# Planner ranks and times, and a few early operations, in an attention and gated-MLP kernel ordered by a list scheduler

## The chip, the cores and the metric

The kernel runs on one core of a Trainium2 chip. The metric is the device time in microseconds (us). One core has TensorE (PE, matrix products; PEld is its weight load), VectorE (DVE), ScalarE (ACT), GpSimd (POOL) and SyncE (SP, which only issues transfers here). Each engine works through its own list of instructions in order, and waits by semaphores for what other engines or transfers deliver.

## What is computed

Eight batches of attention with 8 heads of 64: 32 global rows see all 544 keys, 512 local rows see the 32 global keys and a window of 32 to either side. The result, 4352 rows of 512, goes through two matrix products with a hard-swish gate between them.

```python
k_all = np.concatenate([k_g, k_l], axis=2)
v_all = np.concatenate([v_g, v_l], axis=2)
out_g = np.matmul(sm(scale * q_g @ k_all.T), v_all)             # 32 rows a head
mask = np.abs(pos[:, None] - pos[None, :]) <= 32
s_l = np.concatenate([scale * q_l @ k_g.T, np.where(mask, scale * q_l @ k_l.T, -1e9)], axis=-1)
out_l = np.matmul(sm(s_l), v_all)                               # 512 rows a head
x = np.concatenate([out_g, out_l], axis=2).transpose(0, 2, 1, 3).reshape(8 * 544, 512)
h = x @ w_in                                                    # 512 -> 2048
g = h * np.clip(h + 3.0, 0.0, 6.0) / 6.0
return g @ w_out                                                # 2048 -> 512
```

(shortened; `sm` is a softmax, all in float32)

## The kernel before

**Tiling.** Work goes by batch. q and k are cast to 16 bits and turned so that the head dimension lies on partitions: batch 0 by `stage_loads`, where half comes over SP's queue as float32 and is cast by ScalarE or VectorE (L431), the other half by casting loads from POOL's queue; batch 1 by two casting loads on POOL's queue (into `xt` and `qtmp`); batches 2 to 7 by `wide_loads`. The turns are VectorE transposes in `turn_words` (batches 0 and 1: L590 q, L595 k, L601 and L605 global q and k) and `turn_wide` (the others). The global rows of batches 0 and 1 come through `once`: a load, then four casts each for q and k (L478 and L480). Batch 1's load is issued by SP into `graw0`.

**Local attention** (`local`) handles four groups a batch, each with two units of 32 rows in two halves for all heads: scores (stream `s`, 64 matmuls, L712 for batches 0 and 1, L699 for the rest), mask and row minimum (`mx`, eight VectorE operations, L743), exponentials (`ex`, L749), eight transposes (`t`, L758), their copy from PSUM (`etc`, L318, on either engine), values (`av`, L776), normalisation (`nm`, L785 and L786) and a turn into `xt` (`xp`, L799). The values read `vs`, shifted copies ("strips") of v and of the global v: POOL, ScalarE or VectorE copy them for batch 0, POOL alone for the others (stream `vs`, L540 and L542). `globe` does the 32 global rows.

**Products** (`first`, `second`). For each batch the first product (L907) writes PSUM tiles `m` (three), ScalarE computes the clipped part (`t1`, L918), VectorE multiplies (`gate`, L914) into `gts` and so frees the tile. The second product (L934) works on groups of four matmuls; its result is copied (`ot`) and stored by SP. Batch 0's first product goes over its columns in three parts, of 128, 128 and 256. A batch's attention is held until the first product has come far enough (`hold`).

**Order.** Nothing is issued as the code is read. Every operation goes into a named stream of a `Plan`, with its engine (or a choice of engines), a planned duration, its dependencies and the buffers that it takes and reads. `Plan.lay` is a list scheduler: each stream keeps its own order; among the first operations of all streams it takes the one that can start soonest on its engine, and among those within 0.03 us the one of lowest rank. Where an operation may go on two engines, a free engine that no better-ranked operation wants is taken. The order so found is the order of the instructions on every engine. Planned dependencies fix only this order: at run time an engine waits only for real data dependencies. A load has an issue (on SP, POOL or ACT) and a planned service and flight (`lat`) on one DMA line; at most 8 loads of an engine are out at once. TensorE's operations cost 1.9 times as much before 30 us, and the planner follows its instructions in blocks of 256, of which the next is fetched (L179) while one is worked on:

```python
past = self.count % self.BLOCK + op.n - self.BLOCK
...
return max(0.0, self.fetched - at), at
...
if self.stalls(op, start, cost - self.switch(op))[0] > 0.2:
    rank += 20
```

`n` is the number of instructions: 128 for the scores of one local group in batches 0 and 1, 8 for a group of either product. The streams and their ranks stand at L296, the tiny matmuls that run first (`pad`) at L996. In the code, times of the plan count from its own start, and `when` is the planned time at which a block is used up.

Of the kernel before, what the change touches and what calls it, by code (L numbers as in the profile page):

```python
# [37 lines left out]
class Plan:  # L38
# [83 lines left out]
    def lay(self):  # L122
# [4 lines left out]
        while len(order) < total:  # L127
            found, lone = [], []
            for n, ops in self.streams.items():
                if at[n] == len(ops):  # L130
                    continue
                op = ops[at[n]]
                t = self.ready(op, n)
# [23 lines left out]
            first = min(found)  # L157
# [16 lines left out]
            if e == "PE":  # L174
                wait, when = self.stalls(op, start, self.cost(op, e, start))
                end += wait
                self.mode = op.mode[1]
                if self.count % self.BLOCK + op.n >= self.BLOCK:
                    self.fetched = when + wait + (7.0 if when < 40.0 else 5.2)  # L179
                self.count += op.n  # L180
# [12 lines left out]
def kernel(  # L193
# [102 lines left out]
    for name, rank in (("l0", 0), ("ld", 5), ("lq", -2), ("sh", 0), ("sq", 0), ("st", 3.5), ("g0", 0), ("ga", -9), ("first", -9), ("pad", -30), ("gc", -6), ("gd", 3), ("gp", 3.9), ("cast", -5), ("msk", lambda n: 1 if n < 9 else 1.25), ("tq", lambda n: 0 if n < 8 else 3), ("kg", 0.5), ("vs", 1.5), ("clr", 1),  # L296
                       ("s", 0.5), ("mx", lambda n: 1.2 if n < 33 else 2.7), ("ex", 1.9), ("t", -0.5), ("etc", 0), ("av", -0.7), ("nm", 0.7),
                       ("xp", -0.5), ("gx", 1),
                       ("mf", lambda n: 9 + n * 1e-3), ("ms", lambda n: 9 + (n + len(PARTS) * NDFF + 2) * 1e-3), ("t1", 0), ("gate", -0.7), ("ot", 3)):
        plan.stream(name, rank)  # L300
# [96 lines left out]
    def raw(src, b):  # L397
        return src[b].rearrange("h s d -> (h s d)").rearrange("(c x f) -> x c f", x=P, f=T * D)
# [17 lines left out]

    def stage_loads():
# [3 lines left out]
        there = [[load("g0", "SP", 0.47, 0.65, stage[:, i, c, :], raw(src, 0)[:, c, :], lat=(2.6, 3.1, 3.2, 5.7)[2 * c + i]) for i, src in enumerate((q_l, k_l))]  # L421
# [19 lines left out]
        for m in (2, 3, NU, 1, 0, NU + 1):  # L441
            made["mask", m] = [plan.add("msk", Op(("ACT", 0.21), lambda o=o, i=i: nc.scalar.copy(out=o, in_=i), [lower])) for o, i in places(m)]
# [23 lines left out]
    def once(b, k, src, name):  # L466

        raw_ = (graw0[:, k] if b else ots[k][0:W].rearrange("g (h d) -> g h d", d=D))
        got = load("sh" if b else "ga", "SP" if b else "ACT", 0.47, 0.45 if b else 0.3, raw_, src[b].rearrange("h g d -> g h d"), [w_in_l[1][1]] if b else ())
# [91 lines left out]
    def load_w_in():  # L561

        n = dff // 2
        rows = moe_w_in.rearrange("(k p a) c -> k p a c", k=2, a=2)
        got = [load("l0", "POOL", 0.7, 2.7, w_in_t[i][:, 2 * k:2 * k + 2, :], rows[k, :, :, i * n:(i + 1) * n])
               for i in range(2) for k in range(2)]
        return [got[0:2], got[0:2], got[2:4], got[2:4]]
# [16 lines left out]
    def turn_words(b, st, k):  # L584
# [4 lines left out]
        def turn_q(c0, c1):  # L589
            nc.vector.transpose(out=flat(qt[k.slot])[:, c0:c1].rearrange("p c (q t) -> p c t q", t=T), in_=words(nat(b, 0)[:, c0:c1]))  # L590
# [24 lines left out]
        for q in range(n):  # L615
# [10 lines left out]
            else:  # L626
                st["k"].append(plan.add("tq", Op(("DVE", 1.9 / n), lambda c0=c0, c1=c1: turn_q(c0, c1), st["qk"][q, 0],
                                                 [] if b == 0 else [k])))
                a = plan.add("tq", Op(("DVE", 1.95 / n), lambda c0=c0, c1=c1: turn_k(c0, c1), st["qk"][q, 1]))
                st["k"].append(a)  # L630
# [363 lines left out]
    with tc.manual_schedule():  # L994
        clean = plan.add("first", Op(("DVE", 0.1), lambda: nc.vector.memset(zero, 0.0)))
        plan.add("pad", Op(("PE", 4.0), lambda: [nc.tensor.matmul(out=aps[0][0:W, 0, 0:2], lhsT=zero, rhs=zero[:, 0:2], start=True, stop=True) for _ in range(100)], [clean],  # L996
# [83 lines left out]
```

## Time and profile before

| | |
|---|---|
| time, median of 3 runs | 327.46 us (327.25 to 327.77) |
| the profiled execution | 328.56 us, its span 326.8 us |
| PE busy in the span | 305.8 us (94%), 4484 matmuls |
| DVE, ACT, POOL busy | 258.4 (79%), 238.3 (73%), 157.7 us (48%) |
| mean DMA rate, bytes moved | 121 GB/s, 39.54 MB |
| chain that ended last | PE 86%, POOL 5%, DMA 3%, DVE 2%, issue 2% |
| granted TensorE clock, mean | 0.999 |

The span reaches from the first to the last instruction of one execution; the time of that execution has 1.76 us more around it. Rows of the trace give a start counted from the start of the span, a duration, the engine, the line, the operation, the tiles written and read, and a count; in brackets stands the time for which the engine had been idle before, and what released it. "issue" there means that nothing in the profile explains the wait. PEq, SPq and so on are the instruction queues of the engines.

The first slices of the span, busy time in tenths for each fortieth (8.2 us) of it:

```profile
PE   4477898799999999999999999999999999999995
DVE  7788996789989897989998999889989985742210
ACT  7999678557895788868876997699759965643221
POOL 9999999029955935665009944963900000000000
```

Some transfers at the start, issue and landing in us:

| transfer | queue | issued | to landing |
|---|---|---|---|
| batch 0's staged q and k (four, 256 KB) | SP | 0.73 to 2.13 | 3.2, 3.8, 4.2, 5.5 |
| w_in, four of 512 KB | POOL | 8.17, then 12.61 to 14.75 | 9.2 the first, 10.2 the second, 14.5 the last |
| batch 1's global k, global q (64 KB) | SP | 13.29, 14.12 | 12.2, 14.2 |
| batch 1's q, k (512 KB) | POOL | 19.71, 23.12 | 11.3, 10.5 |
| w_out, four of 512 KB | POOL | 31.69 to 35.61 | 8.2 the first, 13.5 the last |

### The profile page before, as it was taken

Reading aid. Unit: us, or ns where it says so; the run is one execution under the profiler, and the core shown is the slowest. Engines: PE = TensorE matmul, PEld = TensorE weight load, DVE = VectorE, ACT = ScalarE, POOL = GpSimd, SP = SyncE. Lnnn points to the kernel's source line nnn. Section 1 sums busy time; section 2 is a strip of 40 time slices with the busy share of each in tenths; the row PEclk is TensorE's granted clock in tenths of the full one; section 3 lists DMA queues with packets and bytes.
Section 4 is the critical chain, followed back from the end, with each engine's and each line's share of the span. In section 5 each row is a group of like instructions: output and inputs, shape, how many; then the busy total and the mean of one; then the engine's idle time right before and its main releaser. Section 6 shows DMA issues by size and latency. Waiting matters only on the chain.

```text
span 326.8 us, 11215 instructions
## 1 busy us (share of the span) xinstructions
PE 305.8 (94%) x4484; PEld 172.8 (53%) x4484; DVE 258.4 (79%) x913; ACT 238.3 (73%) x550; POOL 157.7 (48%) x205
## 2 busy tenths in 40 slices
PE   4477898799999999999999999999999999999995
PEld 4356784454555545555555555555455545556654
DVE  7788996789989897989998999889989985742210
ACT  7999678557895788868876997699759965643221
POOL 9999999029955935665009944963900000000000
PEclk9999999999999999999999999999999999999999
DMA  8999999959952995199949993999111012011223
GB/s 201 180 215 190 188 212 170 230 152 178 200 85 66 140 184 138 46 111 160 217 118 99 226 138 48 148 157 174 33 35 34 2 34 67 0 34 32 65 53 79
DMA packets 104821, 39.54 MB, mean 121 GB/s; under 512 B 91648, under 2 KB 97536, under 8 KB 104768
## 3 DMA queue, kind: packets, MB, share of 16 engines
q0 software_dynamic: 91392, 16.91, 63.9%
q1 hardware_dynamic: 12832, 21.78, 26.8%
q8 instruction: 35, 0.57, 0.7%
q10 hardware_dynamic: 544, 0.13, 0.2%
q14 instruction: 18, 0.15, 0.2%
HBM read 35.13 MB, written 8.91 MB: 135 GB/s over the span
## 4 chain that ended last, share of the span: by engine, by line
PE 86%; POOL 5%; DMA 3%; DVE 2%; issue 2%; ACT 0%; POOLq 0%
PE m L934 37%; PE m L907 35%; PE t L758 4%; DMA xt<-in_q_l_dram 3%; PE a L776 3%; PE s L699 3%; PE t L847 1%; POOL vs L542 1%; PE s L816 1%; POOL v L308 1%; PE a L857 1%; PE s L712 1%; POOL win L308 1%; DVE qt L590 1%; DVE kt L595 1%
## 5 line engine op out<-in xcount | busy, mean ns | idle before, releaser
L934 PE MATMUL m<-wout,gts 128*128 128x512 f16 (+1 forms) x560 | 130.8, 373 | 1.8 <-issue 1.8
L907 PE MATMUL m<-xt,win 128*128 128x512 f16 (+2 forms) x640 | 121.0, 338 | 2.2 <-DVE gts L914 1.2
L914 DVE SCALAR_TENSOR_TENSOR gts<-t,m 128x512 f16<-128x512 f32 x136 | 92.1, 682 | 34.4 <-ACT t L918 33.1
L918 ACT ACTIVATE t<-m 128x512 f32<-128x512 f32 x136 | 81.2, 597 | 34.5 <-PE m L907 31.4
L907 PEld LDWEIGHTS <-win 128*128 128x128 f16 x704 | 70.4, 114 | 48.0 <-issue 3.8
L542 POOL COPY vs<-v 32x1056 f32<-32x1056 f32 (+4 forms) x91 | 81.7, 898 | 29.1 <-DMA v<-in_v_l_dram 24.8
L749 ACT ACTIVATE ex<-sm,mx 128x128 f16<-128x128 f32 x256 | 84.9, 394 | 7.2 <-DVE mx L743 6.5
L934 PEld LDWEIGHTS <-gts 128*128 128x128 f16 x560 | 51.6, 98 | 52.1 <-issue 3.5
L743 DVE CUSTOM_DVE_ANT_0 sm<-s,mask 128x128 f32<-128x128 f32 x240 | 56.2, 285 | 7.2 <-PE s L712 4.1
L308 POOL DMA_DIRECT2D rawq<-in_q_l_dram x12 | 12.6, 1059 | 46.3 <-DVE rec L785 24.3
L318 ACT COPY et<-t 128x1024 f16<-128x1024 f16 x28 | 28.1, 1005 | 8.1 <-PE t L758 8.0
L308 POOL DMA_DIRECT2D v<-in_v_l_dram x32 | 28.2, 896 | 0.0
L942 ACT COPY ot<-m 128x512 f32<-128x512 f32 (+1 forms) x29 | 16.5, 570 | 15.3 <-PE m L934 15.2
L786 DVE TENSOR_TENSOR x<-a,rec 128x512 f16<-128x512 f32 x32 | 22.1, 692 | 1.1
L799 DVE STREAM_TRANSPOSE xt<-x 128x512 f16<-128x512 f16 x32 | 22.5, 704 | 0.1
L758 PEld LDWEIGHTS <-ex 128*128 128x128 f16 x256 | 17.3, 101 | 9.0 <-ACT ex L749 2.7
L743 DVE DVE_READ_ACCUMULATOR2_ANT mx<- 128x1 f32 x256 | 21.3, 83 | 0.0
L758 PE MATMUL t<-ident,ex 128*128 128x128 f16 x240 | 19.9, 225 | 1.5 <-ACT ex L749 1.5
L318 ACT COPY etg<-t 128x640 f16<-128x640 f16 x16 | 11.1, 692 | 10.5 <-PE t L847 10.5
L776 PEld LDWEIGHTS <-et 128*32 128x32 f16 x1024 | 10.0, 98 | 13.1 <-ACT ex L749 4.7
L646 DVE STREAM_TRANSPOSE qt<-rawq 128x512 f16<-128x512 f16 x24 | 15.5, 680 | 0.0
L650 DVE STREAM_TRANSPOSE kt<-rawk 128x512 f16<-128x512 f16 x24 | 15.5, 679 | 0.0
(92 smaller groups left out, 221.5 us busy)
## 6 DMA issues: line engine op xcount, KB each, us to landing
out_dram<-ot SPq DMA_DIRECT2D x62, 128.0 KB, 2.9
vs<-vg SPq DMA_DIRECT2D x32, 132.0 KB, 5.4
v<-in_v_l_dram POOLq DMA_DIRECT2D x32, 128.0 KB, 6.4
rawq<-in_q_l_dram POOLq DMA_DIRECT2D x12, 256.0 KB, 5.8
rawk<-in_k_l_dram POOLq DMA_DIRECT2D x12, 256.0 KB, 6.8
rawq<-rawq SPq DMA_DIRECT2D x12, 254.0 KB, 5.3
rawk<-rawk SPq DMA_DIRECT2D x12, 254.0 KB, 4.9
win<-in_moe_w_in_dram POOLq DMA_DIRECT2D x4, 512.0 KB, 11.3
```

What stands on the lines that cost most here:

```text
L308: eng.dma_start(out=o() if callable(o) else o, in_=i() if callable(i) else i)
L318: nc.scalar.copy(out=o(), in_=i())
L542: (nc.gpsimd if op.engine == "POOL" else nc.vector).tensor_copy(out=o(), in_=i())
L743: nc.vector.tensor_tensor_reduce(out=sms[sm.slot], in0=scored(c // 2)[:, z:z + P], in1=mask(m), scale=-scale, scalar=3.0e38, op0=ALU.add, ...
L749: nc.scalar.activation(out=exs[ex.slot][:, un, c, :], in_=sms[sm.slot], func=EXP, scale=-1.0, bias=mxs[mx.slot])
L758: nc.tensor.matmul(out=turned(tp)[:, z:z + P], lhsT=exs[ex.slot][:, un, c, :], rhs=ident, is_transpose=True)
L786: nc.vector.tensor_tensor(out=xs[x.slot].rearrange("p g (a d) -> p g a d", a=2), in0=o[:, :, 0:D].rearrange("p g (d a) -> p g a d", a=2), ...
L799: nc.vector.transpose(out=xts[xt.slot][:, :, n * P:(n + 1) * P].rearrange("p k (t q) -> p t k q", q=W), in_=xs[x.slot].rearrange("p (t k) ...
L907: nc.tensor.matmul(out=mps[ps.slot][:, k * n:(k + 1) * n], lhsT=column_tile(c)[:, m], rhs=x, start=(m == 0), stop=(m == KC - 1))
L914: nc.vector.scalar_tensor_tensor(out=g, in0=shape(t1s[t1.slot][:, 0:all_]), scalar=1.0, in1=shape(mps[ps.slot][:, 0:all_]), op0=ALU.min, o ...
L918: r = plan.add("t1", Op(("ACT", 0.09 + all_ * 0.00083), lambda: nc.scalar.activation(out=t1s[t1.slot][:, 0:all_], in_=mps[ps.slot][:, 0:al ...
L934: nc.tensor.matmul(out=mps[ps.slot][:, 0:n], lhsT=gfn(c), rhs=w_out_t[c // 4][:, c % 4, cols], start=(c == 0), stop=(c == NDFF - 1))
```

## The change

1. `pad` is planned with 1.45 us in place of 4.0; the last staged load of batch 0 with a flight of 4.9 in place of 5.7; w_in's loads with a service of 2.6 in place of 2.7.
2. The fourteen mask copies of `stage_loads` may go on ScalarE (0.18) or VectorE (0.11); before, on ScalarE alone (0.21).
3. In `once`, batch 1's two global loads get a POOL memset of one column of their destination ahead of them (stream `gm`, rank 1.0), which is planned after w_in's last load. Since the memset writes where the load will write, SP's load waits for it. Before, the load had a planned dependency on w_in's second load and no real one.
4. In `turn_words`, batch 1's turn of q, one operation, and its turn of k, one operation of four instructions, become four operations each, by pairs of heads. Batch 0 keeps its pieces; the planned cost becomes 0.03 + 0.48 or 0.49 a piece.
5. After a block of instructions used up between 40 and 62 us of the plan, the next is planned 6.2 us later in place of 5.2.
6. Ranks: `vs` 1.5 to 2.2, `s` 0.5 to 1.2, `mx` 1.2 and 2.7 to 0.5 and 2, `ex` 1.9 to 1.2, `t` -0.5 to 0.2, `nm` 0.7 to -0.7, `gate` -0.7 to -1.4.

```diff
-                    self.fetched = when + wait + (7.0 if when < 40.0 else 5.2)
+                    self.fetched = when + wait + (7.0 if when < 40.0 else 6.2 if when < 62.0 else 5.2)
...
-    ("gd", 3), ("gp", 3.9), ... ("vs", 1.5), ("clr", 1),
-    ("s", 0.5), ("mx", lambda n: 1.2 if n < 33 else 2.7), ("ex", 1.9), ("t", -0.5), ("etc", 0), ("av", -0.7), ("nm", 0.7),
+    ("gd", 3), ("gm", 1.0), ("gp", 3.9), ... ("vs", 2.2), ("clr", 1),
+    ("s", 1.2), ("mx", lambda n: 0.5 if n < 33 else 2), ("ex", 1.2), ("t", 0.2), ("etc", 0), ("av", -0.7), ("nm", -0.7),
...
-    ("t1", 0), ("gate", -0.7), ("ot", 3)):
+    ("t1", 0), ("gate", -1.4), ("ot", 3)):
...
+    def mask_part(o, i, lower):
+        op = Op({"ACT": 0.18, "DVE": 0.11}, None, [lower])
+        op.emit = lambda: nc.scalar.copy(out=o, in_=i) if op.engine == "ACT" else nc.vector.tensor_copy(out=o, in_=i)
+        return plan.add("msk", op)
...
-    lat=(2.6, 3.1, 3.2, 5.7)[2 * c + i]
+    lat=(2.6, 3.1, 3.2, 4.9)[2 * c + i]
...
-            made["mask", m] = [plan.add("msk", Op(("ACT", 0.21), lambda o=o, i=i: nc.scalar.copy(out=o, in_=i), [lower])) for o, i in places(m)]
+            made["mask", m] = [mask_part(o, i, lower) for o, i in places(m)]
...
-        got = load("sh" if b else "ga", ..., src[b].rearrange("h g d -> g h d"), [w_in_l[1][1]] if b else ())
+        after = [plan.add("gm", Op(("POOL", 0.1), lambda: nc.gpsimd.memset(raw_[:, 0, 0:1], 0.0), [w_in_l[3][1]]))] if b else ()
+        got = load("sh" if b else "ga", ..., src[b].rearrange("h g d -> g h d"), after)
...
-        got = [load("l0", "POOL", 0.7, 2.7, w_in_t[i]...
+        got = [load("l0", "POOL", 0.7, 2.6, w_in_t[i]...
...
-                st["k"].append(plan.add("tq", Op(("DVE", 1.9 / n), lambda c0=c0, c1=c1: turn_q(c0, c1), st["qk"][q, 0],
-                                                 [] if b == 0 else [k])))
-                a = plan.add("tq", Op(("DVE", 1.95 / n), lambda c0=c0, c1=c1: turn_k(c0, c1), st["qk"][q, 1]))
-                st["k"].append(a)
+                pieces = [(c0, c1)] if b == 0 else [(c, c + 1) for c in range(c0, c1)]
+                for x, y in pieces:
+                    st["k"].append(plan.add("tq", Op(("DVE", 0.03 + 0.48 * (y - x)), lambda x=x, y=y: turn_q(x, y), st["qk"][q, 0],
+                                                     [k] if b and x == c0 else [])))
+                for x, y in pieces:
+                    a = plan.add("tq", Op(("DVE", 0.03 + 0.49 * (y - x)), lambda x=x, y=y: turn_k(x, y), st["qk"][q, 1]))
+                    st["k"].append(a)
...
-        plan.add("pad", Op(("PE", 4.0), ...
+        plan.add("pad", Op(("PE", 1.45), ...
```

## The prediction

> **What bounds the kernel now.** I read the busy time by stretch first. Columns: stretch, its length, busy us and instructions of each engine, TensorE clock, DMA share, GB/s.
>
> ```profile
> 30.00:40.00 10.00, 7.67 (x181) 7.07 (x179) 9.79 (x19) 7.23 (x15) 9.19 (x16) 1.00 1.56 179
> 40.00:50.00 10.00, 10.00 (x205) 8.64 (x203) 10.00 (x45) 7.97 (x20) 9.35 (x10) 1.00 1.48 208
> 50.00:60.00 10.00, 7.23 (x191) 3.73 (x189) 5.86 (x38) 7.53 (x21) 7.25 (x9) 1.00 2.17 179
> 60.00:70.00 10.00, 10.00 (x185) 5.34 (x184) 8.22 (x19) 5.72 (x11) 0.00 (x0) 1.00 1.06 232
> 70.00:100.00 30.00, 30.00 (x417) 15.39 (x416) 27.47 (x104) 23.92 (x55) 23.59 (x26) 1.00 1.16 137
> ```
>
> From 60 us to 300 us TensorE is busy the whole time, in every stretch. What is left there is a fixed amount of matmul, so the time can change only by what TensorE loses before 60 us, or by a new hole behind it. Second, the chain of waits from 20 to 60 us (start, length, what), which names those losses.
>
> ```profile
> 19.71 11.34 DMA xt<-in_q_l_dram
> 31.08 2.08 DVE qt L590
> 33.15 1.20 DVE gts L914 x2
> ...
> 35.20 1.98 DVE kt L595 x4
> 37.18 0.53 DVE gts L914
> ...
> 37.75 4.69 PE m L907 x56
> ```
>
> Batch 1's q lands at 31.05; VectorE turns all of it in one piece, then k, and the gates (L914), which free the PSUM tiles of the first MoE product, come between and behind. The last gate lets TensorE go on. Third, TensorE in order of time (start, length, line, what, count, idle before it and its releaser).
>
> ```profile
> 37.75 4.69 PE L907 MATMUL m<-xt,win 128*128 128x128 f16 x56 [1.22 <-DVE gts L914]
> ...
> 51.34 0.63 PE L712 MATMUL s<-kt,qt 32*32 32x128 f16 x51
> 52.89 0.30 PE L712 MATMUL s<-kt,qt 32*32 32x128 f16 x13 [0.92 <-issue]
> 53.12 1.04 PE L934 MATMUL m<-wout,gts 128*128 128x512 f16 x4
> 53.99 0.61 PE L758 MATMUL t<-ident,ex 128*128 128x128 f16 x8
> 54.44 1.03 PE L934 MATMUL m<-wout,gts 128*128 128x512 f16 x4
> 55.40 0.42 PE L776 MATMUL a<-vs,et 128*32 128x65 f16 x32
> 55.75 0.74 PE L712 MATMUL s<-kt,qt 32*32 32x128 f16 x64
> 56.42 0.82 PE L934 MATMUL m<-wout,gts 128*128 128x512 f16 x3
> 59.09 1.25 PE L934 MATMUL m<-wout,gts 128*128 128x512 f16 x5 [1.85 <-issue]
> ```
>
> Two holes have no releaser but "issue", and both fall inside a run of equal matmuls (51 and 13 of 64; 3 and 5 of 8). From the end of the first to the second there are 13+4+8+4+32+64+3 = 128 matmuls, each with its weight load: 256 instructions, the planner's BLOCK. So TensorE waits for its next block of instructions; from resuming to resuming it is 59.09 - 52.89 = 6.20 us. Two earlier holes of this kind end at 26.69 and 32.67 (5.98 apart, 127 matmuls). The planner counts 5.2 from 40 us on, 7.0 before.
>
> The Trainium skill, page "Runtime: NRT & Kernel Launch", section "Instruction fetch mechanics", says that the sequencer fetches the next 256 instructions while it executes the current ones and that this is mostly hidden. By it the holes would be no fetches, edit (4) below would gain nothing, and the sum would be 1.3 us in place of 3.0 (327.46 - 1.3 = 326.2). The trace agrees on the 256, but not on the hiding: 0.92 and 1.85 us stand there. I go by the trace.
>
> **The change, part by part.** Sums are against the profiled execution: 328.56 us, span 326.8, so 1.76 outside it. The median, 327.46, is 1.10 below; I take differences off the median.
>
> (1) Start: pad's true cost (the trace has 2.82 us for it; the planner had 4.0, made longer by its cold factor), the last staged load 4.9, masks on either engine, exponentials ahead of strips on ScalarE (ex 1.2 under vs 2.2). No work leaves. Now ScalarE copies eight masks (7.08 to 8.34) and a 0.40 us cast ahead of the last cast of k, at 8.68, though its load landed at 2.13 + 5.5 = 7.63. VectorE waits 1.25 us for it and TensorE 2.63. Masks taken by VectorE let it start up to 8.68 - 7.63 = 1.05 us sooner. ScalarE's strips from 11.69 to 14.86 hold the exponentials up to 1.5 us. Above, the gain ends where the first MoE matmul (24.11) meets w_in (second load, 12.61 + 10.2 = 22.8): 1.3. Below: a mask copy on VectorE isn't in the trace; between a 32x32 memset (0.09) and the 32x256 cast of gn (0.38), 14 of them cost 1.3 to 5.3 us; VectorE's idle time in the first 20 us is 5.6, so at worst -0.5. I take **0.5**, under half, as the later stages have their own waits.
>
> (2) Global rows held. Two POOL memsets (0.10 each, like the 32x16 one at 10.03) follow w_in's planned landing; SP's two loads wait for them, and behind them on SP only batch 1's vs strips, which wait for vg until 33.96 anyway. Moved past: w_in's last two loads and q and k of batch 1. 128 KB at 205 GB/s is 0.62 us that those land sooner. VectorE was idle only 0.11 us before q's turn: **0.1**. The rows land later: issued at about 28.7 (w_in's last load: 14.04 + 14.5 = 28.5), and taking 3.5 us (ScalarE's first such load) to 14.2 (this load now), so 32.2 to 42.9. Needed: eight casts of 0.40 on two engines, then the turn of global k at 41.19. By SP's own strips at that time (7.2 to 10 us) it is 36 to 39: in time. Bounds: 0.1 and -3.4 (42.9 + 1.7 casts + 0.74 turn + 0.5 to the scores at 42.37). This is the rival below.
>
> (3) Quarters, gate first (-1.4). k's turn is four instructions already (2.06 us); q's 2.08 becomes four of 0.52 back to back, or 0.64 alone: up to 0.5 us more VectorE work. What moves is the gates: ScalarE's halves from 34.10 were done by 35.42, their gates began at 37.04 behind k's turn, and TensorE stood 1.22 us. Gates between quarters remove that; the turn of global k (41.19) stays, as VectorE is full either way. Bounds: -0.5, and 1.22 + 0.67 (the fetch hole at 32.0, if its block fills better) = 1.9. I take **0.8**. Late next: w_out's fourth load, 35.1 + 13.5 = 48.6, needed 2.6 us after the second product starts (48.2), so starting 1.2 sooner is covered.
>
> (4) Fetch at 6.2 from 40 to 62 us. An operation that the planner sees stall over 0.2 us gets rank +20, so a second-product group (8 instructions, 0.86 us) goes first. The block comes no sooner; the hole is filled with work from behind. Full: 0.92 + 1.85 = 2.77. Limit: batch 1's first product (69.98) needs its last turned x, which ends at 68.2 + 0.7 = 68.9, so 1.1 is free at once; more if the 1.25 us of second product at 59.09, ahead of a transpose at 60.63, moves into the hole: 1.1 + 1.25 = 2.35. I take two whole groups, **1.7**; bounds 0 and 2.77.
>
> (5) The other ranks. Engine by engine the order of the streams hardly changes: TensorE keeps av, t, s, MoE; VectorE keeps gate first and gets nm ahead of xp, etc and early turns, early mx ahead of gx. Hidden by TensorE's full stretches: **0**, bounds -0.5 to 0.5 (five mode switches of 0.1: 0.97 against 0.86 for a group behind a switch).
>
> Sum 0.5 + 0.1 + 0.8 + 1.7 = 3.1, less 0.1 for the memsets: 3.0. **327.46 - 3.0 = 324.5** (span 323.8).
>
> **Rivals.**
> R1, holes move: MoE work put into the holes is missing later, TensorE waits for batch 1's last x at 68.9, and the quarters gain nothing, VectorE being full from 30 to 50. For: the busy 9.79 and 10.00 above; 128 matmuls need 6.2 us whatever they are, and batch 1's attention is made of small ones. Against: TensorE still had second-product work until 69.7. Gain 1.1 at most, with the start's 0.5 half lost: **326.5**; in a third of it under 0.65.
> R2, slower: the global rows come too late. The planner gives a load some 2 us of flight after its service; this queue shows 7 to 14. POOL's four casts stand at 32.77 ahead of w_out's last two loads and batch 1's strips. If the rows land at 28.7 + 8 = 36.7, POOL stands 3.9 us: w_out's last lands at 48.6 + 3.9 = 52.5 against 50.8 when its matmuls come, strips end at 53.35 + 3.9 = 57.3 against 55.40 for the first values. TensorE loses 1.7 to 1.9: 327.46 + 1.9 = **329.4**. It decides from a landing later than about 34.8 with casts where they stand. Against: casts have rank 3.9, behind those loads, and 41.19 leaves room.
> R3, planning doesn't cure the holes: the "issue" idle comes from something else, or the real times lie too far from the planned ones. For: the two earlier holes were planned with 7.0, longer than the 6.0 seen, and came all the same. Against: the counts of 127 and 128. Then (4) is 0 and the rest 3.0 - 1.7 = 1.3: **326.2**. That is what the page would give.
>
> **Chances.** Forecast 0.48 (own range 322.4 to 326.1: the sum's terms within some two thirds of their bounds), R1 0.14, R2 0.30, R3 0.08. The measurement tells 0.2%, 0.65 us, from no change. Faster: 0.48 x 0.98 + 0.14 x 0.6 + 0.08 x 0.7 = 0.61; slower 0.30 and a little of R1: 0.31; same 0.08. The gains' upper bounds give 1.3 + 0.1 + 1.9 + 2.77 = 6.1 (321.4); I end the range at 322.0. Above I end at R2 nearly, 329.3.
>
> **What would show it.** Right: no "issue" hole over 0.5 us on TensorE between 45 and 62 us, more L934 before 60; L914 between pieces of L590 and L595, and no 1.22 us wait at L907; graw issued after 24 us; L431's last cast by 8.2; batch 1's first L907 at about 67. Wrong: graw landing after 37 with POOL or ScalarE idle before L480 or L478; L934 waiting for wout; TensorE idle between 62 and 75 for xt; any idle behind 75, which I count at nothing.

## The result, and the profile after

The changed kernel is slower: 339.1 us (median of 4 runs, 337.3 to 342.1) against 327.62 us for the kernel before, run beside it, a ratio of 1.035 (95% interval 1.031 to 1.039). The profiled execution took 339.68 us, its span 337.9, which is 11.1 us more than the span of before. In the code after, lines behind the first additions are counted higher: L478 and L480 (casts of the global rows) are L484 and L486, L590 and L595 (turns) are L596 and L601, L907, L914, L918 and L934 (products and gates) are L916, L923, L927 and L943.

The busy time by stretch, same columns as before, shows where it went.

```profile
30.00:40.00 10.00, 4.95 (x137) 4.43 (x121) 6.32 (x13) 2.81 (x6) 2.54 (x6) 0.95 1.52 183
40.00:50.00 10.00, 5.34 (x67) 5.24 (x68) 4.20 (x9) 4.96 (x10) 6.75 (x10) 0.53 1.15 173
50.00:60.00 10.00, 10.00 (x204) 8.53 (x202) 9.60 (x43) 8.30 (x23) 9.45 (x12) 1.00 1.64 107
60.00:70.00 10.00, 10.00 (x226) 5.38 (x223) 5.87 (x27) 7.59 (x18) 6.16 (x7) 1.00 0.91 108
70.00:100.00 30.00, 27.71 (x423) 14.14 (x412) 25.75 (x88) 21.73 (x49) 18.27 (x21) 0.94 1.24 167
```

Between 30 and 50 us TensorE, VectorE, ScalarE and POOL stand together: TensorE is busy 10.3 us of 20 (17.7 before), ScalarE 7.8 (15.2 before), and the granted clock falls to 0.53 in the second stretch. From 50 to 70 TensorE is full, the 7.23 of before is gone. Then 2.3 us are missing between 70 and 100. The chain of waits names the first stand (start, length, what).

```profile
31.86 0.14 POOL graw L474 x2
32.00 11.00 DMA graw<-in_k_g_dram
43.07 0.09 ACT gn L484
...
43.92 0.70 ACT etg L318
44.66 0.47 PE a L866 x20
...
79.05 0.10 DVE kt L659
79.69 0.68 DVE xt L808
80.41 1.87 PE m L916 x4
```

The two memsets run at 31.86. The held load of the global k is issued at 32.00 and lands 11.0 us later; ScalarE waits for it (L484), and behind ScalarE's copy `etg` stand TensorE's values of the global rows (L866) and the first product. How both cast engines came to wait is seen in ScalarE's and POOL's operations in order of time (idle time before an operation and its releaser in brackets).

```profile
32.21 0.60 ACT L927 ACTIVATE t<-m 128x512 f32<-128x512 f32 x1
43.07 0.82 ACT L484 CAST gn<-graw 32x256 f16<-32x256 f32 x2 [10.26 <-DMA graw<-in_k_g_dram]
43.92 0.69 ACT L318 COPY etg<-t 128x640 f16<-128x640 f16 x1
...
32.39 0.54 POOL L308 DMA_DIRECT2D wout<-in_moe_w_out_dram  x1 [0.39 <-issue]
43.12 0.83 POOL L486 CAST gn<-graw 32x256 f16<-32x256 f32 x2 [10.20 <-DMA graw<-in_k_g_dram]
```

Since the planner gave the load 2 us, it put two casts on ScalarE and two on POOL close behind its issue. On ScalarE the next operations are the copy `etg` (L318) and `t1` (L927); on POOL the rest of w_out and batch 2's q and k. TensorE's list shows what that did.

```profile
44.66 0.41 PE L866 MATMUL a<-v,etg 128*32 128x65 f16 x16 [9.71 <-ACT etg L318]
45.06 7.93 PE L916 MATMUL m<-xt,win 128*128 128x128 f16 x72
...
80.41 3.38 PE L916 MATMUL m<-xt,win 128*128 128x512 f16 x8 [1.19 <-DVE xt L808]
```

TensorE stands 9.71 us, and the 72 matmuls behind it take 110 ns each, against 84 in the run of 56 before: 72 x 26 ns = 1.9 us more. The clock in short stretches (the third number from the end) falls while TensorE stands, and comes back only some time after work starts again:

```profile
38.00:40.00 2.00, 0.00 (x0) 0.00 (x0) 0.00 (x0) 0.00 (x0) 0.00 (x0) 0.78 1.06 195
40.00:42.00 2.00, 0.00 (x0) 0.00 (x0) 0.00 (x0) 0.00 (x0) 0.00 (x0) 0.50 1.07 188
48.00:50.00 2.00, 2.00 (x22) 1.99 (x20) 1.45 (x3) 0.91 (x2) 2.00 (x3) 0.67 1.92 148
50.00:52.00 2.00, 2.00 (x21) 2.00 (x19) 1.65 (x5) 1.68 (x5) 1.84 (x5) 1.00 2.42 161
```

At 80.41 there is a second, smaller stand of 1.19 us, and the eight matmuls of 512 columns behind it take 3.38 us in place of 1.89 (half clock again). POOL's loads of batch 2 were issued from 44.4 us for q and 47.4 for k (35.6 and 38.9 before); so SP's second copy that spreads k (`rawk` to `rawk`) comes late too. In SP's queue, in order of time:

```profile
73.66 0.54 SPq L308 DMA_DIRECT2D rawk<-rawk  x1
```

Before, it was issued at 61.69. It takes 5.2 us to land, at 78.9, and at 79.05 VectorE starts the turn that reads it (L659), which stands ahead of the last turn of batch 1's x (L808, 79.69), and that one ahead of the first product at 80.41. (The full chain names a copy of `vs` that landed at 78.99, within 0.1 us of this one; L659 reads k.)

**Progress against before.** For the experiments I use one table. Every matmul is given a fixed cost by its form, and the costs are summed as a run proceeds; the entry is the time at which a run has done a given sum, less the time at which before had done it (the left column). Positive is later, in us. It is worked out from TensorE's records of one profiled execution of each kernel. The execution of before is itself 1.1 us above the median, and the last experiments show that up to about 1.5 us of an entry at 60.7 can be this execution and not the edit.

```
before's   after  no    hold  fetch no hold, ranks quart. start ranks + no hold,
time              hold  alone alone no fetch alone alone  alone quart.  two parts
 24.94      0.40  0.38  0.09  0.39   0.37    0.36  0.83  -0.07  -0.04    0.37
 39.81      9.80 -0.26 11.71  0.39  -0.30    2.96  0.93   0.84  -0.22   -0.31
 50.10      9.82  0.19 11.90  1.41   0.11    4.97  1.08   2.89   0.21    0.13
 60.70      6.48 -3.38  8.50 -1.99  -3.41    1.58 -1.88  -0.51  -3.35   -3.43
 66.89      6.27 -3.36  8.51 -1.81  -3.40    1.58 -1.69  -0.50  -2.03   -3.29
 72.82     10.45  1.21  8.68  0.22   0.93    1.75 -1.65  -0.33   0.88   -2.90
147.71     11.02  2.11  9.61  1.63   1.19    2.75 -0.57   0.61   1.29   14.89
317.84     11.14  2.54 11.23  1.64   3.19    4.19 -0.21   2.06   1.40   21.91
```

In the changed kernel 9.8 us are lost by before's 40, 3.3 are regained between 50 and 61, and 4.2 are lost again between 67 and 73. Little happens after that.

### The profile page after: what moved, and what is told of

It is laid out like the page before. It is cut to its first block, busy times and chain, and to the rows that moved or that the text cites. A ratio compares the mean times of both kernels' runs of the same rounds, so it can differ in the third digit from the quotient of the medians.

```text
span 337.9 us, 11223 instructions
## 1 busy us (share of the span) xinstructions
PE 309.6 (92%) x4484; PEld 175.1 (52%) x4484; DVE 259.1 (77%) x925; ACT 238.9 (71%) x543; POOL 156.9 (46%) x205
## 4 chain that ended last, share of the span: by engine, by line
PE 84%; POOL 9%; DMA 4%; issue 1%; ACT 0%; DVE 0%; POOLq 0%; ACTq 0%; DVEq 0%
PE m L916 36%; PE m L943 35%; PE t L767 4%; DMA graw<-in_k_g_dram 3%; POOL vs L548 3%; PE a L785 3%; PE s L708 2%; POOL v L308 2%; PE s L825 1%; PE t L856 1%; PE a L866 1%; PE s L721 1%; POOL wout L308 1%; POOL win L308 1%; DMA vs<-vg 1%
## 5 line engine op out<-in xcount | busy, mean ns | idle before, releaser
L943 PE MATMUL m<-wout,gts 128*128 128x512 f16 (+1 forms) x560 | 131.2, 373 | 0.0
L923 DVE SCALAR_TENSOR_TENSOR gts<-t,m 128x512 f16<-128x512 f32 x136 | 92.3, 683 | 50.5 <-ACT t L927 49.3
L916 PE MATMUL m<-xt,win 128*128 128x512 f16 (+2 forms) x640 | 127.4, 347 | 1.2 <-DVE xt L808 1.2
L927 ACT ACTIVATE t<-m 128x512 f32<-128x512 f32 x136 | 81.0, 597 | 37.9 <-PE m L916 36.5
L548 POOL COPY vs<-v 32x1056 f32<-32x1056 f32 (+5 forms) x89 | 80.9, 909 | 38.9 <-DMA v<-in_v_l_dram 34.6
L916 PEld LDWEIGHTS <-win 128*128 128x128 f16 x704 | 72.0, 117 | 46.0 <-issue 3.8
L943 PEld LDWEIGHTS <-gts 128*128 128x128 f16 x560 | 52.0, 98 | 51.8 <-issue 1.7
L318 ACT COPY et<-t 128x1024 f16<-128x1024 f16 x30 | 30.2, 1006 | 8.2 <-PE t L767 8.1
L951 ACT COPY ot<-m 128x512 f32<-128x512 f32 (+1 forms) x31 | 17.7, 571 | 14.7 <-PE m L943 14.4
L308 POOL DMA_DIRECT2D rawq<-in_q_l_dram x12 | 12.6, 1059 | 30.9 <-DMA vs<-vg 11.1
L808 DVE STREAM_TRANSPOSE xt<-x 128x512 f16<-128x512 f16 x32 | 22.4, 700 | 0.1
L318 ACT COPY etg<-t 128x640 f16<-128x640 f16 x16 | 11.1, 694 | 8.5 <-PE t L856 8.5
L659 DVE STREAM_TRANSPOSE kt<-rawk 128x512 f16<-128x512 f16 x24 | 15.3, 674 | 0.6 <-DMA vs<-vg 0.6
```

Source lines behind the costliest of these rows:

```text
L308: eng.dma_start(out=o() if callable(o) else o, in_=i() if callable(i) else i)
L318: nc.scalar.copy(out=o(), in_=i())
L548: (nc.gpsimd if op.engine == "POOL" else nc.vector).tensor_copy(out=o(), in_=i())
L808: nc.vector.transpose(out=xts[xt.slot][:, :, n * P:(n + 1) * P].rearrange("p k (t q) -> p t k q", q=W), in_=xs[x.slot].rearrange("p (t k) ...
L916: nc.tensor.matmul(out=mps[ps.slot][:, k * n:(k + 1) * n], lhsT=column_tile(c)[:, m], rhs=x, start=(m == 0), stop=(m == KC - 1))
L923: nc.vector.scalar_tensor_tensor(out=g, in0=shape(t1s[t1.slot][:, 0:all_]), scalar=1.0, in1=shape(mps[ps.slot][:, 0:all_]), op0=ALU.min, o ...
```

## The experiments

All ratios are against the kernel before, run beside the edited one on the same chip, with the 95% interval in brackets. My theory after the result was that the held load alone is the loss, because of casts that stand where it was planned to land, and that the rest of the change is level or a small gain. The rivals were that the load's lateness hurts wherever the casts stand (then a true planned flight would not cure it), and that the other parts lose by themselves.

### The held load: taken out, alone, and with a true flight

Taken out of the changed kernel:

```diff
-        after = [plan.add("gm", Op(("POOL", 0.1), lambda: nc.gpsimd.memset(raw_[:, 0, 0:1], 0.0), [w_in_l[3][1]]))] if b else ()
+        after = [w_in_l[1][1]] if b else ()
```

> The changed kernel with batch 1's global rows loaded as before (no memset, planned behind w_in's second load); all other edits stay. Theory A (the held rows land 11 us after their issue, behind casts planned for 2 us, and ScalarE and POOL stand there): the 9.7 us hole of TensorE and the half clock behind it are gone, 324.5 to 327 us by the other edits. Theory B (the other edits, ranks and quarters, cost time themselves): 330 us or more, with new holes of TensorE at other places.

Measured: 333.45 us against 328.02, ratio 1.017 (1.013 to 1.022). The profiled run has no stand of four engines, as theory A has it, but the time is theory B's. So the hold makes some 6 of the 11.5 us here, and the other edits together lose 5.4 us, where I had them level or gaining. Alone, as the only edit to the kernel before:

```diff
-        got = load("sh" if b else "ga", ..., src[b].rearrange("h g d -> g h d"), [w_in_l[1][1]] if b else ())
+        after = [plan.add("gm", Op(("POOL", 0.1), lambda: nc.gpsimd.memset(raw_[:, 0, 0:1], 0.0), [w_in_l[3][1]]))] if b else ()
+        got = load("sh" if b else "ga", ..., src[b].rearrange("h g d -> g h d"), after)
```

> The kernel before with the hold alone: two memsets on POOL, planned behind w_in's last load, ahead of batch 1's two global loads. Theory A: the rows land at 42 to 44 us, ScalarE or POOL idle for 8 to 10 us ahead of their casts, TensorE idle for 6 to 10 us, 335 to 340 us. Theory B: 327 to 329 us, since POOL's memsets cost 0.2 us and the rows are needed only by the turn at 41 us.

Measured: 339.73 us, ratio 1.036 (1.032 to 1.041): theory A, and as slow as the whole change. ScalarE, POOL and TensorE in order of time in this kernel:

```profile
44.20 0.82 ACT L479 CAST gn<-graw 32x256 f16<-32x256 f32 x2 [11.95 <-DMA graw<-in_k_g_dram]
44.25 0.83 POOL L481 CAST gn<-graw 32x256 f16<-32x256 f32 x2 [10.85 <-DMA graw<-in_k_g_dram]
46.68 0.86 PE L848 MATMUL t<-ident,eg 128*128 128x128 f16 x5 [11.51 <-ACT eg L837]
```

The same three waits, here with ScalarE's exponentials of the global rows (`eg`) behind the casts. Third, the hold stays and only the planner is told how long the load flies:

```diff
-        got = load(..., after)
+        got = load(..., after, lat=11.0 if b else 2.0)
```

> The changed kernel with the hold, but the planner counts 11.0 us of flight for batch 1's global rows in place of 2.0; no work changes, only the order. Theory A1 (the loss is the place of the casts, not the lateness): the casts stand behind the landing at about 43 us, ScalarE and POOL idle under 2 us ahead of them, 326.5 to 330 us (scores of batch 1 some 3.5 us later than the 42.4 of before, mostly hidden by MoE work). Theory A2 (the lateness itself costs, since batch 1's scores can't start): 334 us or more.

Measured: 334.18 us, ratio 1.017 (1.011 to 1.023). That is the time of A2 and not of A1; but the kernel without the hold takes as long, so what is left is not the lateness. The load is again issued at 32.0 and flies 11.1 us, but the casts, all eight on ScalarE in this order, now stand where it has landed, and have no wait in front:

```profile
43.49 0.41 ACT L484 CAST gn<-graw 32x256 f16<-32x256 f32 x1
```

So the late landing itself costs nothing that these runs can tell (each interval is some 0.5% to either side). The order planned for a landing that never came costs the difference to the changed kernel, and even in the right order the hold gains nothing that shows. The casts changed place and, in part, engine; which of the two counts more was not told apart.

### Fetch times alone, and the change without hold and without fetch

```diff
-                    self.fetched = when + wait + (7.0 if when < 40.0 else 5.2)
+                    self.fetched = when + wait + (7.0 if when < 40.0 else 6.2 if when < 62.0 else 5.2)
```

> The kernel before with the next block of instructions planned 6.2 us later between 40 and 62 us, nothing else. By the prediction's term: the 0.92 and 1.85 us holes of TensorE get second-product groups, 325.9 us (1.7 less than before), at best 324.8. Rival (the holes move, or planning misses them): 327.2 to 328 us, with issue holes of 0.5 us or more still between 45 and 65 us, or TensorE waiting for batch 1's x near 69 us.

Measured: 329.16 us, ratio 1.004 (1.001 to 1.007): no gain, as the rival has it, and a little worse than its time. TensorE in order of time has no hole left between 45 and 60, but these two elsewhere:

```profile
41.80 2.05 PE L907 MATMUL m<-xt,win 128*128 128x256 f16 x17 [0.95 <-issue]
...
71.57 1.02 PE L907 MATMUL m<-xt,win 128*128 128x512 f16 x4 [1.79 <-DVE xt L799]
```

By the table it leads by 2.0 us at 60.7, and is 0.2 behind at 72.8: the second-product groups that filled the holes are missing when batch 1's last x is awaited. For the next kernel, the changed one with the hold and this line undone, one theory was that the fetch edit moved the last scores of batch 1, so that without it they would come at 56 to 58 us.

> The changed kernel without the hold and with 5.2 us for the next block of instructions as before; start, quarters and ranks stay. Theory C (the longer fetch makes the planner run second-product groups too early, so that batch 1's scores come late and TensorE stands for its x near 70 us): the last L721 of batch 1 is back at 56 to 58 us (62.6 with the fetch edit), the waits behind 66 us are gone, 327 to 329.5 us. Theory D (start, quarters and ranks are at fault): 332 us or more.

Measured: 331.95 us against 328.43, ratio 1.011 (1.009 to 1.013), about the time of theory D. The last scores of batch 1 come at 61.69, so theory C fell. By the table this kernel and the one with the fetch edit keep step to 67 us (-3.40 and -3.36): no hole of "issue" stands at 50 to 60 here either, though the planner counts 5.2. What it shows behind the wait near 70 is the clock, in a row of TensorE and two short stretches:

```profile
71.43 3.11 PE L916 MATMUL m<-xt,win 128*128 128x512 f16 x8
...
70.00:72.00 2.00, 1.29 (x7) 0.74 (x8) 2.00 (x5) 1.41 (x4) 0.60 (x1) 0.63 0.80 183
72.00:74.00 2.00, 2.00 (x7) 0.66 (x5) 1.19 (x3) 0.90 (x2) 1.50 (x2) 0.52 0.73 61
```

Behind waits of only 0.59 and 1.19 us (ending at 68.71 and 70.71) the clock is half, at a cost of 3.11 - 1.89 = 1.2 us. In the kernel without the hold the profiled run kept the clock (mean 1.0) and is the fastest of six, 331.08 us; the other five, 332.5 to 335.1, have means of 0.990 to 0.995. That the same half clock near 70 us makes them slower is likely, not seen, as only one run has a trace.

### The other parts alone

The ranks (the diff's three lines of part 6) as the only edit:

> The kernel before with the new ranks alone. By the prediction's term (their order hardly differs): 327.1 to 328.5 us, within 0.2% of before. Theory D: 329.5 us or more, from exponentials ahead of strips on ScalarE or from normalisations ahead of turns on VectorE.

Measured: 332.2 us against 328.43, ratio 1.013 (1.010 to 1.015): theory D. TensorE, then VectorE, in order of time:

```profile
36.21 0.61 PE L907 MATMUL m<-xt,win 128*128 128x128 f16 x8 [1.25 <-DVE gts L914]
39.28 4.24 PE L907 MATMUL m<-xt,win 128*128 128x128 f16 x40 [1.48 <-DVE gts L914]
...
29.32 0.68 DVE L320 COPY et<-m 128x1024 f16<-128x1024 f16 x1
32.95 0.69 DVE L786 TENSOR_TENSOR x<-a,rec 128x512 f16<-128x512 f32 x1
33.55 2.08 DVE L590 STREAM_TRANSPOSE qt<-xt 128x1024 f32<-128x1024 f32 x1
```

VectorE takes the copy and the normalisation of batch 0 first, and its turn of q starts at 33.55 in place of 31.08. Two waits for gates (1.25 and 1.48 us) stand where one of 1.22 was, and TensorE has a hole of "issue" of 1.73 us at 54.19. The quarters of part 4 alone:

> The kernel before with batch 1's turns of q and k in quarters alone. By the prediction's term: the 1.22 us wait of TensorE for the gate near 37 us is gone, 326.3 to 327.3 us. Rival (VectorE is full from 30 to 50 us, so nothing is gained, or the turns end later and batch 1 with them): 327.5 to 330 us.

Measured: 328.72 us, ratio 1.001 (0.999 to 1.004): the rival, nothing gained. One wait for a gate of 1.05 us remains, with another of 0.45. Yet the table has this kernel 1.9 us ahead at 60.7, because the two "issue" holes at 52.89 and 59.09 are not there, without any change to the fetch times (how far holes vary by themselves is shown below). The start (parts 1 and 2) alone:

> The kernel before with the start's edits alone (pad 1.45, last staged load 4.9, w_in 2.6, masks on either engine). By the prediction's term: 326.8 to 327.3 us. Theory D1 (VectorE's eight mask copies of 0.20 us, in place of the planned 0.11, stand ahead of the first turn): first scores at 8.0 to 8.4 us (6.78 before), first L907 0.3 to 0.6 us later, 328.3 to 329.5 us.

Measured: 331.85 us, ratio 1.011 (1.008 to 1.013). The first scores come at 8.24 us (6.78 before), as theory D1 has it, behind eight mask copies that VectorE now makes in 1.65 us (most of 0.18, one of 0.60); but at 25 us the kernel is level again, and by 50 us it is 2.9 us behind, so the loss is larger than D1's and comes later. The mask copies alone (`mask_part` and its call):

> The kernel before with the fourteen mask copies on either engine, nothing else. If VectorE's copies (0.20 us each in place of the planned 0.11) ahead of the first turns are the start's cost: 330 us or more, first scores near 8.2 us. If the cost lies in the other three planned numbers, or in the order that follows: 327.5 to 329 us.

Measured: 327.62 us against 327.84, ratio 0.999 (0.996 to 1.001), though the first scores come at 8.22 here too. So the masks by themselves cost nothing, and the start's 1.1% comes only with its planned numbers (1.45, 4.9 and 2.6), through the order that they make. Which of the three it is, and whether the masks have a part in it then, was not told apart. Ranks and quarters together:

> The kernel before with the new ranks and the quarters. If the ranks cost because normalisations and copies of et go ahead of the 2.08 us turns and gates then stand behind these (two waits of TensorE of 1.25 and 1.48 us at 36 and 39 us with the ranks alone), the quarters mend it: 328 to 330 us, waits under 0.9 us there. If not: 331.5 us or more.

Measured: 332.12 us, ratio 1.011 (1.006 to 1.015): the time for "if not". The quarters do mend what the ranks spoil at 40 to 50 us (0.21 in place of 4.97 in the table), but not the time; the lead of 3.35 at 60.7 is that of the changed kernel without its hold. That lead is gone at 72.8.

### Filling the wait at 70 us

If the lead is lost because TensorE has to wait for all of batch 1's x, the first product of batch 1 in two parts, each needing half of the turned x, should keep it.

```diff
+    parts_of = lambda b: PARTS if b == 0 else ((0, 1), (2, 3)) if b == 1 else (tuple(range(NJ)),)
...
-            st["xt"] = Buf("xt", NDFF * (len(PARTS) if b == 0 else 1))
+            st["xt"] = Buf("xt", NDFF * len(parts_of(b)))
...
-        for at, part in enumerate(PARTS if b == 0 else [range(NJ)]):
+        for at, part in enumerate(parts_of(b)):
```

(the rank of `mf` is counted in half steps for batch 1; the program has 4548 matmuls in place of 4484, as 64 of 512 columns become 128 of 256). On the changed kernel without its hold:

> The changed kernel without the hold, with batch 1's first product in two parts of 256 columns (as batch 0's last part is), so that it may start when half of batch 1's x is turned. Theory C (what the fetch edit, the quarters and the ranks gain by 67 us, 3.4 us, is given back because TensorE waits for batch 1's last x, since the MoE work put into the holes is missing then): the stretch from 66 to 73 us fills up, 327.5 to 329.5 us, 4 us below the run without the two parts. Rival (the loss behind 67 us is of another kind): 331.5 us or more, as without the two parts.

Measured: 350.41 us against 327.65, ratio 1.070 (1.067 to 1.072): far above theory C and above the time without the two parts (333.45), which the rival meant; the slowest kernel of all. TensorE in order of time:

```profile
72.87 3.30 PE L917 MATMUL m<-xt,win 128*128 128x256 f16 x28
...
103.28 0.94 PE L944 MATMUL m<-wout,gts 128*128 128x512 f16 x3 [1.92 <-issue]
107.51 0.63 PE L786 MATMUL a<-vs,et 128*32 128x65 f16 x32 [1.16 <-ACT et L319]
```

The wait at 70 us is gone and the lead still 2.9 us at 72.8, as the theory has it; but then TensorE uses up its work sooner and meets batch 2's attention, which is no earlier. From 100 to 112 us it is busy 7.6 us of 12, and the granted clock is 0.50 from 104 to 112; by 148 us it is 14.9 behind. On the kernel before, the same two parts:

> The kernel before with batch 1's first product in two parts, nothing else. Theory C: before, TensorE still had second-product work until 69.7 us when the last x came at 68.9, so there is nothing to fill: 327 to 329 us. If it gains over 1 us, the wait for x bound the kernel before too.

Measured: 329.12 us, ratio 1.007 (1.004 to 1.010): no gain by itself, as theory C has it. With the quarters, the fetch times and `pad` at 1.45, without the hold, the ranks and the rest of the start:

> The kernel before with the quarters, the fetch at 6.2 us and batch 1's first product in two parts; start and ranks as before, no hold. Theory C: the gains of the two edits (1.8 us each by 67 us) are kept, 324.5 to 327 us, faster than before. Rival (other losses come behind 80 us, as in every edited kernel so far): 327.5 to 329.5 us.

Measured: 332.21 us, ratio 1.015 (1.011 to 1.019), slower than both forecasts. This one leads by 2.5 us until about 97 us and loses 3.6 at 100 to 107, in waits for batch 2's attention, the longest (1.51 us at 107.45) for its x: the same loss, one batch further on.

### How much any other order costs

Three kernels change one planned number of the kernel before by a little, which changes no work, only the order that the planner finds.

```diff
-            st["k"].append(plan.add("tq", Op(("DVE", 2.8 / QPARTS), lambda h=h: turn_q(h, h + n), st["qk"][0],
+            st["k"].append(plan.add("tq", Op(("DVE", 2.75 / QPARTS), lambda h=h: turn_q(h, h + n), st["qk"][0],
```

> The kernel before with one planned cost of no meaning changed: the turns of batches 2 to 7 planned with 2.75 in place of 2.80 us (the trace has 2.45 for the four). The work is the same and so is the order until batch 1 is done; behind it the order of all engines is another. Theory E (the order of before was found for this very plan, and any other order loses 1 to 2 us at the later batches): 328.7 to 330.5 us. Rival (the late losses of the edited kernels come from their edits): 327.5 to 328.5 us, as before.

```diff
-        st["xT", n] = plan.add("xp", Op(("DVE", 0.7), xturn, done, new, [x]))
+        st["xT", n] = plan.add("xp", Op(("DVE", 0.71), xturn, done, new, [x]))
```

> The kernel before with the planned cost of the turn of x at 0.71 in place of 0.70 us (the trace has 0.70): the same work in another order from early on. Theory E (any other order of the plan loses): 329.5 us or more. Rival (meaningless changes of the plan cost little, so the 1.1 and 1.3% are the edits' own): 327.5 to 328.8 us.

```diff
-    LATE = (2.0, 4.0, 7.0) + (9.0,) * (B - 3)
+    LATE = (2.0, 4.0, 7.2) + (9.0,) * (B - 3)
```

> The kernel before with batch 2's loads planned with 7.2 in place of 7.0 us of flight: the same work, another order from batch 2 on. Theory E: 329 us or more. Rival: 327.5 to 328.6 us.

Measured: 328.04, 329.7 and 328.7 us, ratios 1.003 (1.001 to 1.005), 1.006 (1.003 to 1.009) and 1.002 (0.998 to 1.005). Theory E's time came in the second alone, and the third cannot be told from no change. So an order that nobody meant cost nothing to 0.6%, up to 2 us, in three tries. The fetch edit's 0.4% cannot be told from that; the ranks' and the start's 1.1 to 1.3% lie above all three. No kernel that I ran beats the one before; the one with the masks alone is level with it.

These three show one thing more. Up to 98 us the order on TensorE, VectorE, ScalarE and POOL is that of before in all three (with 0.71 too, where I expected another from early on), so a hole before 60 us that the order makes should be the same. TensorE at the place where before has 1.85 us of "issue" (59.09), in the kernels with 2.75, 7.2 and 0.71:

```profile
58.01 1.25 PE L934 MATMUL m<-wout,gts 128*128 128x512 f16 x5 [0.75 <-issue]
...
58.48 1.25 PE L934 MATMUL m<-wout,gts 128*128 128x512 f16 x5 [1.30 <-issue]
...
56.90 2.00 PE L934 MATMUL m<-wout,gts 128*128 128x512 f16 x8
```

With the same order the second hole is 1.85, 1.30, 0.75 or some 0.1 us; the first stays at 0.77 to 1.05. The profiled execution of before happened to have the largest.

## Why the prediction was wrong

**The step that failed is (2), the held global rows.** I took the landing at 36 to 39 ("in time") and a gain of 0.1. The issue was at 32.0, not 28.7, because POOL's list has the memsets behind other transfers, and the flight was 11.0 us where I took 7.2 to 10: the landing, 43.0, is the upper end that I had worked out (42.9) and set aside. The price at that end was mis-sized too. I followed the rows through the turn of k to the scores (-3.4 us), as if only the work that needs the rows could be late. What was late first was everything behind the casts on ScalarE's list, the copy `etg` and all of `t1`, and so TensorE: 9.71 us of standing in place of the 1.22 of before, and 1.9 us at half clock, together 10.4, near the 9.8 that the table shows. The kernels with the hold alone, without it and with the true flight show this cause.

It is not the whole miss. Without the hold the change still loses 1.7%, 5.4 us, where the terms that are left, (1), (3) and (4), add up to a gain of 3.0; the profiled runs differ by 2.5 of these 5.4, and the rest, likely half clock near 70 us, stays open.

**R2, the rows come too late, is the rival that came**, by its mechanism but not its size: +1.9 forecast, 11.5 us measured. I priced POOL's queue alone. ScalarE idle before L478 stood among my signs of being wrong, and four of the eight casts were on ScalarE already before (28.48 and 32.60), but I put no price on its list, which feeds every gate. My argument against it, that 41.19 leaves room, looked at when the data are needed; what counts is when the engine reaches the instruction.

**Steps (1), (3) and (4): the sum of 3.0 us seemed to hold to 67 us, and no further.** Without the hold the kernel leads by 3.36 us at before's 66.9 us, of which up to 1.5 may be before's own large hole; that it is so near 3.0 is in part luck. R1 said what comes then, a wait for batch 1's last x, and I gave it 0.14: the second product has run out at 67.8, where before it went on to 69.7 with eight matmuls left over, and until the last turn of x ends at 72.8 TensorE has only small pieces of attention, with waits between. TensorE, and then one line of VectorE, in order of time in the kernel without the hold (L943 is the second product, L833 and L856 the global rows, L916 batch 1's first product):

```profile
67.38 0.38 PE L943 MATMUL m<-wout,gts 128*128 128x512 f16 x1 [0.73 <-issue]
69.20 0.45 PE L833 MATMUL s<-kt,qg 32*32 32x288 f16 x16 [0.99 <-ACT eg L846]
72.10 0.71 PE L856 MATMUL t<-ident,eg 128*128 128x128 f16 x5 [1.19 <-ACT eg L845]
72.83 1.89 PE L916 MATMUL m<-xt,win 128*128 128x512 f16 x8
...
72.11 0.67 DVE L808 STREAM_TRANSPOSE xt<-x 128x512 f16<-128x512 f16 x1
```

From 66 to 72 us TensorE is busy 2.73 us of 6. I had forecast that product at about 67; it came at 72.83, and at 80.41 in the changed kernel. The two-part kernels show that the loss at 70 us is this wait, and that filling it in this way only sends it on to batch 2, larger there. So "the time can change only by what TensorE loses before 60 us" was the wrong reading of a full stretch: it was full because its work was enough to cover the waits for attention, by little.

**Step (4) took one execution's holes for a fixed loss.** Alone the edit leads by 1.8 us at 66.9 us (1.7 forecast), but the kernel with the turn of x at 0.71, whose order there is that of before, also lacks the second hole, worth up to 1.85 us. From resuming to resuming the same block took 6.20 us in before and 5.10, 5.65 and 4.28 in the three nudged kernels, so no one planned number fits it. The holes also vanish with the quarters alone and in the kernel without fetch edit and hold, so the terms do not add. R3 was right in its second half (the real times lie too far from the planned ones): with the fetch edit and the true flight a hole of 1.42 us stands at 61.32. Its first half fell; the holes are waits for instructions, as the last section shows.

**Step (3):** four quarters of q take 2.12 us together, with 0.5 to 0.7 us for one, as I took. Gates do go between the pieces of k, as forecast, and the wait of 1.22 us goes to 0.24; VectorE's list in the kernel without the hold:

```profile
38.03 0.67 DVE L601 STREAM_TRANSPOSE kt<-qtmp 128x256 f32<-128x256 f32 x1
38.54 0.68 DVE L923 SCALAR_TENSOR_TENSOR gts<-t,m 128x512 f16<-128x512 f32 x1
...
39.35 0.62 DVE L601 STREAM_TRANSPOSE kt<-qtmp 128x256 f32<-128x256 f32 x1
```

It takes the quarters and the ranks together; with quarters alone 1.05 us of the wait stay.

**Step (5) was wrong:** "hardly changes" and 0 (at most 0.5) against 1.3% alone, 3.8 us. VectorE is not hidden at 30 to 40 us, as its 9.79 of 10 said: the normalisation that I noted as moving ahead moved q's turn back by 2.5 us. **Step (1)** was a gain of 0.5 and alone loses 1.1%, 3.4 us: the masks move as planned and the last staged cast starts at 8.19 in place of 8.68, as forecast, but the first scores come at 8.23 in place of 6.78, since VectorE makes masks first. At 25 us the start alone is 0.07 us ahead, and the whole change 0.40 behind. The start's loss comes after that: in the kernel with the start alone TensorE waits 1.57 us for a gate at 38.59 and 1.75 us for VectorE's `mx` at 52.20. Which of its numbers makes that order stays open.

## What to carry to other kernels

A load that is moved must be planned with the flight measured at the place that it is moved to, and the price of its being late is counted on every in-order engine that may hold a consumer, by what stands behind it there and not by when the data are needed. A hole that is filled with later work is a gain only if that work was not covering a later wait: before adding up such gains, look for what the next batch's data would do one hole earlier. A list-scheduled kernel is first nudged by numbers that mean nothing; here three such nudges cost up to 0.6%, and a forecast below that is no forecast. The nudged kernels also give the holes of one and the same order several times over: a hole that is 1.85 us in one profile and 0.1 in the next is not a loss that a plan can fill.

## What the hardware showed

**A small load beside large ones.** The 64 KB of one load of global rows flew 11.0 us in the changed kernel, at the 173 to 183 GB/s that the stretches above show. Its packets are 256 B, those of w_out on POOL's queue 4096 B. Counted by the us in the transfers' records (records of 4 B left out):

```
after, us        36-37  37-38  38-39  39-40  40-41
SP, 256 B           44     52     54     48     38   (about 30 ns each)
POOL, 4096 B        45     48     48     41     41   (320 to 420 ns each)
```

The counts are nearly one for one, so the small load gets some 47 x 256 B = 12 KB a us (an estimate from these counts) while the large ones get 15 times as much. Before, the same load flew 12.2 us, from 20 to 24 us beside packets of 2048 B, again nearly one for one (74 to 93 against 84 to 89 a us). The Trainium skill, page "DMA: Bandwidth & Descriptors", section on the queues and their arbitration, says that an engine takes turns between its queues packet by packet; the equal counts from 36 to 41 us agree with it. They do not hold from 32 to 35 us: after its issue none of the load's packets moved, while POOL's queue moved packets of 128 B (batch 1's v), 1179, 611 and 175 a us; why is open. So in both flights the time went to what the other queue carried, and holding the load until w_in was there did not shorten it by more than 1.2 us: v and w_out were under way by then.

**The clock.** TensorE stood from 44.66 - 9.71 = 34.95 us. If the clock is either whole or half, the 0.78 of the stretch from 38 to 40 means half from 39.1, 4.2 us after the stand began; the 0.67 from 48 to 50 means whole from 49.3, 4.7 us after the matmuls resumed (an estimate from these two stretches). The Trainium skill, page "TensorE: Matmul & The Clock Gate", in the part on what is actually happening, gives half rate after an idle window of about 3.4 us; this stand agrees roughly. The one near 70 us does not look like it: in the kernel without hold and fetch edit waits of 0.59 and 1.19 us, with small attention matmuls between them, stood ahead of 0.52 in the next 2 us. The same page, in its part on a second failure mode, has a clock that swings where TensorE idles briefly and often, which is nearer; what decides it here no run tells, as the kernel without the hold kept 1.00 in the traced run through waits of the same size.

**Blocks of instructions.** The trace also records the transfers that bring instructions. In before, one queue carries 35 of 16384 B; 35 x 256 is 8960, and TensorE has 4484 matmuls and as many weight loads, 8968. One lands at 51.32 and the next at 57.67 us, and TensorE resumes 1.57 and 1.42 us later, at 52.89 and 59.09. In the three nudged kernels the second of these lands at 56.50, 56.37 and 56.97, and TensorE resumes 1.51, 1.27 and 1.51 us later. So the two holes are waits for a block of instructions, and when it lands varies from execution to execution with the order unchanged; what delays it no run tells.
